# Storing the last tile of a fused attention and feed-forward kernel by column halves

## The chip, the core and the metric

The kernel runs on one core of a Trainium2 chip. A core has a matrix engine (PE, TensorE) with its own queue for weight loads (PEld), a vector engine (DVE), a scalar engine (ACT), GpSimd (POOL) and a queue engine (SP, SyncE). PE writes its results to PSUM, in banks of 128 partitions by 512 float32. DVE and ACT read PSUM and write SBUF. DMA transfers move data between SBUF and HBM; here they are issued from SP's queue and, a few of them, from ACT's queue, and they run on the core's 16 DMA engines. The metric is the device time of one execution in microseconds (us), the median of several runs.

## The reference

A small attention (8 batches, 8 heads, 576 tokens, 64 channels) over 32 learned slots per head is followed by a feed-forward layer with an ELU:

```python
def _attn_ref(q, k, v, phi):
    a = softmax(phi, axis=2)                      # over the 576 tokens
    k_m = np.einsum('bhsm,bhsd->bhmd', a, k)      # 32 slots per head
    v_m = np.einsum('bhsm,bhsd->bhmd', a, v)
    attn = softmax(q @ k_m.T / 8, axis=-1)
    return attn @ v_m

def _moe_ref(x, w_in, w_out):                     # x: 4608 x 512
    h = x @ w_in                                  # 512 -> 2048
    g = np.where(h > 0.0, h, np.exp(np.minimum(h, 0.0)) - 1.0)
    return g @ w_out                              # 2048 -> 512
```

## The kernel before, in words

The tokens of a batch are worked on in two halves of 288. `hidden` makes 128 of the 2048 feed-forward channels for one half (a PSUM tile `psh` of 128 x 288), ACT and DVE apply the ELU, and `project` multiplies the result by 128 rows of `w_out` and adds it up over the 16 groups of channels (j = 0 to 15) in PSUM banks `pso`. Every product is made of three passes over high and low parts of the operands (`PASSES`), to keep float32 precision; `by_channels` issues the three matmuls of one group.

A half has 288 tokens, that is two tiles of 128 (NT = 2) and 32 left over (REST). `project` takes the two tiles. The 32 left-over tokens are gathered: two batches, two halves each, make 4 x 32 = 128 rows, one full tile `rest` for each pair of batches (p = 0 to 3). When a pair is through, eight units (i = 0 to 7) run, each for two groups of channels: `rest_high` (ACT) and `rest_low` (DVE) split the values into high and low parts `gp`, and `rest_project` (PE) issues six matmuls of 128 x 512 into one bank, `pso00`. `rest_store` then copies the bank to an SBUF tile `orest` on ACT and stores it to `out`. Its 128 rows lie in `out` as four blocks of 32 rows (batch b, half h), each block contiguous, the blocks 288 rows apart. The stores of p = 0, 1 and 2 stand in the middle of the program, that of p = 3 is the last thing that the kernel does.

The order is written by hand: the list `FIRST` for the first part and a table of places (`at(place, step, ...)`, sorted by place) for the rest; each engine runs its instructions in that order. For the last pair, the eight units stand at it + 0.612 to it + 0.682, the copies of the last two ordinary tiles (`collect`) at it + 0.7, their store at it + 0.8 and `rest_store` at it + 0.81.

Two other lines matter for the reading. `store` (L950) writes two ordinary tiles with one transfer of 128 partitions (512 KB). `spread_max` (L282) sends eight rows of 128 B to a DRAM tile `nmd`; its destination is written as four rows of two pieces (`d.rearrange("a r x -> r a x")`, that is 4 x 2 x 32 elements).

Of the kernel before, what the change touches and what calls it, by code (L numbers as in the profile page):

```python
# [12 lines left out]
ALU = mybir.AluOpType  # L13
# [3 lines left out]
P = 128  # L17
B, H, S, D, M = 8, 8, 576, 64, 32
DM, DFF = 512, 2048
HALF = S // 2  # L20
NT = HALF // P
REST = HALF - NT * P
# [9 lines left out]
NJ = DFF // P  # L32
# [142 lines left out]
def fused_kernel(ctx: ExitStack, tc: tile.TileContext, phiT, phi, kv0, kvt, kv, kvb, q0, q1, w_in, w_out, out):  # L175
# [8 lines left out]
    nc = tc.nc  # L184
# [13 lines left out]
    wout = {}  # L198
    def t2k(shape, name):
        return work.tile(shape, F32, name=name, tag="t2k", bufs=7)  # L200
# [47 lines left out]
    def bank(shape, where):  # L248

        pool, name = {  # L250
            "b": (ps_b, "psb"), "h": (ps_h, "psh"),
            "w": (ps_o, "pso00"), "x": (ps_o, "pso01"),
            "y": (ps_o, "pso10"), "z": (ps_o, "pso11"),
        }[where]
        return pool.tile(shape, F32, name=name)
# [578 lines left out]
    gs = {}  # L834
# [75 lines left out]
    acc = {}  # L910
    osbs = {}

    def by_channels(ps, gp, j, first, last):
        for n, (x, y) in enumerate(PASSES):
            nc.tensor.matmul(  # L915
                ps,
                gp[:, y],
                wout[j][:, x, :],
                start=(first and n == 0),
                stop=(last and n == 2),  # L920
            )

    def project(it):
        b, hf, j = order[it]
        _, first, last = ends[it]
        if first:
            acc[b, hf] = [ps_o.tile([P, DM], F32, name=f"pso{hf}{t}") for t in range(NT)]
        gp = gps.pop(it)
        for t in range(NT):
            by_channels(acc[b, hf][t], gp[:, :, t * P : (t + 1) * P], j, first, last)  # L930
# [31 lines left out]
    def rest_low(p, i):  # L962
# [2 lines left out]
            gp[:, LO], gf.rearrange("p j n -> p (j n)"), gp[:, HI], ALU.subtract  # L965
        )

    def rest_project(p, i):
        if i == 0:
            acc["rest", p] = ps_o.tile([P, DM], F32, name="pso00")  # L970
        gp = gs.pop(("rest", p, i))[1]
        for n in range(2):
            j = 2 * i + n
            by_channels(acc["rest", p], gp[:, :, n * P : (n + 1) * P], j, j == 0, j == NJ - 1)

    def rest_store(p):
        t = t2k([P, DM], "orest")
        nc.scalar.copy(t, acc.pop(("rest", p)))

        eng = (nc.sync, nc.scalar) if p == B // 2 - 1 else (nc.sync, nc.sync)  # L980
        for n in range(4):
            eng[n % 2].dma_start(
                out[2 * p + n // 2, n % 2, NT * P :], t[n * REST : (n + 1) * REST, :]
            )

    tiny = work.tile([P, 1], F32, name="tiny", bufs=1)
    work.tile([P, 24], F32, name="pad_tiny", bufs=1)
# [22 lines left out]
    def warm_up(n):  # L1010
# [8 lines left out]
        for f in (  # L1019
# [4 lines left out]
            softmax_divide, back, turn_back, probs_high, probs_low, vw, vw_high, vw_low, hidden,  # L1024
            elu_exp, elu_max, elu_rest, rest_copy, elu_high, elu_low, project, collect, store, rest_high, rest_low,
            rest_project, rest_store,
        )
    }
    words = {"K": (0,), "V": (1,), "KV": (0, 1)}
    first = []  # L1030
# [9 lines left out]
    def at(place, f, *a):  # L1040
        if (f, a) not in done:
            plan.append((place, len(plan), f, a))
# [84 lines left out]
    for it, (b, hf, j) in enumerate(order):  # L1127
        o = it - 1.35 if it in behind else it - 1.7
        if b > NB:
            o -= 0.96 * (it % 2)  # L1130
        at(o, hidden, it)
        at(o + 0.01, elu_exp, it)
        at(o + 0.02, elu_max, it)
        if b < NB:
            at(it - 1.67, rest_copy, it)
        elif b > NB and b % 2 == 0 and order[max(it - 2, 0)][0] != b:
            at(32 * b - 0.34 + 0.005 * (it - 32 * b), elu_rest, it)
        else:
            at(o + 0.03, elu_rest, it)
        late = 0.695 if it and b != order[it - 1][0] and b % 2 == 0 and b > NB else 0  # L1140
        at(it - 1 + late, elu_high, it)
        at(it - 0.99 + late, elu_low, it)
        at(it + 0.6, project, it)
        if ends[it][2]:
            for t in range(NT):
                at(it + 0.7, collect, it, t)
            if j == NJ - 1:
                at(it + 0.8, store, b, hf)
                if b % 2 and hf:
                    for i in range(NJ // 2):  # L1150
                        at(it + 0.61 + 0.01 * i, rest_high, b // 2, i)
                        at(it + 0.611 + 0.01 * i, rest_low, b // 2, i)
                        at(it + 0.612 + 0.01 * i, rest_project, b // 2, i)
                    at(it + 0.81, rest_store, b // 2)

    plan.sort(key=lambda x: x[:2])
# [50 lines left out]
```

## Time and profile before

| | us |
|---|---|
| median of 3 runs (701.78 to 702.86) | 702.29 |
| the profiled execution | 702.28 |
| its span, from the first to the last instruction | 700.3 |
| PE busy in it | 690.1 |
| DVE, ACT, POOL busy | 460.1, 445.5, 66.2 |

The profiled execution's time is 1.98 us longer than its span. The profile lists the instructions by engine and source line, the waits between them, the chain of work that ended last, and the packets of the DMA engines: a packet is one contiguous piece that one engine moves, or the 4-byte write with which an engine reports that its part of a transfer is done. The share of the DMA engines is an average over all 16.

### The profile page before, as it was taken

Reading aid. Unit: us, or ns where it says so; the run is one execution under the profiler, and the core shown is the slowest. Engines: PE = TensorE matmul, PEld = TensorE weight load, DVE = VectorE, ACT = ScalarE, POOL = GpSimd, SP = SyncE. Lnnn points to the kernel's source line nnn. Section 1 sums busy time; section 2 is a strip of 40 time slices with the busy share of each in tenths; the row PEclk is TensorE's granted clock in tenths of the full one; section 3 lists DMA queues with packets and bytes.
Section 4 is the critical chain, followed back from the end, with each engine's and each line's share of the span. In section 5 each row is a group of like instructions: output and inputs, shape, how many; then the busy total and the mean of one; then the engine's idle time right before and its main releaser. Section 6 shows DMA issues by size and latency. Waiting matters only on the chain.

```text
span 700.3 us, 14400 instructions
## 1 busy us (share of the span) xinstructions
PE 690.1 (99%) x5496; PEld 579.7 (83%) x5496; DVE 460.1 (66%) x1264; ACT 445.5 (64%) x1106; POOL 66.2 (9%) x111
## 2 busy tenths in 40 slices
PE   8999999999999999999999999999999999999997
PEld 7778887888868888888887887888888888878886
DVE  4989887977696558576664666766674655766442
ACT  3879988877457576656655566655664555666552
POOL 0332352123001010001000010000100000000000
PEclk9999999999999999999999999999999999999999
DMA  9992014341404451123202232030501200000001
GB/s 337 407 364 91 1 42 143 101 146 42 137 31 134 168 181 47 49 85 120 85 1 60 90 112 92 31 103 3 174 29 46 69 1 31 1 31 1 30 1 46
DMA packets 24220, 64.14 MB, mean 92 GB/s; under 512 B 3288, under 2 KB 4824, under 8 KB 24152
## 3 DMA queue, kind: packets, MB, share of 16 engines
q1 hardware_dynamic: 23480, 63.06, 25.8%
q8 instruction: 44, 0.72, 0.4%
q10 hardware_dynamic: 672, 0.16, 0.1%
q14 instruction: 24, 0.20, 0.1%
HBM read 53.77 MB, written 9.44 MB: 90 GB/s over the span
## 4 chain that ended last, share of the span: by engine, by line
PE 94%; DMA 4%; DVE 0%; issue 0%; ACT 0%; SPq 0%
PE pso L915 57%; PE psh L854 29%; PE psb L578 3%; PE psb L505 2%; DMA raw<-w_out 2%; PE pso L578 2%; DMA raw<-w_in 1%; PE psh L578 1%; DMA qh<-q 1%; DMA touch<-kv 0%; PE psb L591 0%; PE pso L591 0%; PE psb L547 0%; PE psh L734 0%; SPq L321 0%
## 5 line engine op out<-in xcount | busy, mean ns | idle before, releaser
L915 PE MATMUL pso<-wout,gp 128*128 128x512 f32 x1728 | 426.8, 393 | 0.0
L915 PEld LDWEIGHTS pso<-wout,gp 128*128 128x128 f32 x1728 | 314.2, 188 | 66.5 <-issue 4.0
L854 PEld LDWEIGHTS psh<-A,vw 128*128 128x128 f32 x1536 | 218.4, 188 | 19.4 <-DVE gp L907 2.5
L854 PE MATMUL psh<-A,vw 128*128 128x288 f32 x1536 | 230.4, 295 | 0.7 <-ACT A L777 0.4
L869 ACT ACTIVATE gf<-psh 128x288 f32<-128x288 f32 x256 | 104.6, 409 | 120.8 <-PE psh L854 118.0
L881 DVE SCALAR_TENSOR_TENSOR gf<-gf,psh 128x256 f32<-128x256 f32 x192 | 80.3, 418 | 115.9 <-ACT gf L870 115.8
L907 DVE TENSOR_TENSOR gp<-gf,gp 128x256 fp32r<-128x256 f32 x256 | 113.2, 445 | 29.0 <-ACT gp L901 27.0
L901 ACT CAST gp<-gf 128x256 fp32r<-128x256 f32 x256 | 101.5, 401 | 34.1 <-DVE gf L881 17.3
L870 ACT ACTIVATE gf<-gf 128x288 f32<-128x288 f32 x256 | 113.9, 445 | 8.1
L293 POOL TENSOR_TENSOR e<-e,nmb 128x512 f32<-128x512 f32 (+1 forms) x18 | 19.1, 1081 | 291.9 <-DMA e<-phi 97.6
L878 DVE SCALAR_TENSOR_TENSOR gf<-gf,psh 128x288 f32<-128x288 f32 x64 | 28.5, 450 | 17.1 <-ACT gf L870 15.4
L889 DVE SCALAR_TENSOR_TENSOR rest<-gf,psh 128x32 f32<-128x32 f32 x192 | 34.6, 180 | 0.0
L816 DVE TENSOR_TENSOR vw<-psb,vw 128x512 fp32r<-128x512 f32 (+2 forms) x40 | 20.9, 561 | 14.3 <-ACT vw L810 14.3
L959 ACT CAST gp<-rest 128x256 fp32r<-128x256 f32 x32 | 13.0, 406 | 25.1 <-PE pso L915 25.1
L964 DVE TENSOR_TENSOR gp<-rest,gp 128x256 fp32r<-128x256 f32 x32 | 13.3, 421 | 18.8 <-ACT gp L959 18.5
L897 POOL COPY rest<-gf 128x32 f32<-128x32 f32 x64 | 18.7, 319 | 71.2 <-DVE gf L878 71.2
L810 ACT CAST vw<-psb 128x512 fp32r<-128x512 f32 (+2 forms) x40 | 17.5, 488 | 11.8 <-PE psb L578 11.6
L395 ACT ACTIVATE mag<-raw 128x512 uint32<-128x512 uint32 x30 | 20.0, 669 | 2.7 <-DVE win L417 1.4
L391 ACT ACTIVATE mag<-raw 128x512 f32<-128x512 f32 x30 | 19.7, 667 | 1.3 <-DMA raw<-w_in 1.0
L578 PE MATMUL psb<-win,kvm 64*32 64x512 f32 (+2 forms) x320 | 17.9, 505 | 0.0
L816 DVE TENSOR_TENSOR vw<-pso,vw 128x512 fp32r<-128x512 f32 (+1 forms) x18 | 10.1, 597 | 9.9 <-ACT vw L810 9.8
L505 PEld LDWEIGHTS psb<-kvt,e 64*32 64x32 f32 x864 | 12.6, 105 | 3.3 <-issue 3.3
(144 smaller groups left out, 474.1 us busy)
## 6 DMA issues: line engine op xcount, KB each, us to landing
kvt<-kvb SPq DMA_DIRECT2D x24, 512.0 KB, 4.8
raw<-w_in SPq DMA_DIRECT2D x15, 512.0 KB, 8.0
raw<-w_out SPq DMA_DIRECT2D x15, 512.0 KB, 10.0
out<-osb SPq DMA_DIRECT2D x14, 512.0 KB, 2.8
qt<-q SPq DMA_DIRECT2D x18, 384.0 KB, 4.3
kvt<-kv SPq DMA_DIRECT2D x8, 512.0 KB, 8.9
ph<-phiT SPq DMA_DIRECT2D x7, 576.0 KB, 5.6
e<-phi SPq DMA_DIRECT2D x12, 256.0 KB, 3.4
```

The lines of the kernel that those rows point to most:

```text
L505: nc.tensor.matmul(ps[a][32 * j : 32 * j + 32], e[r, 32 * j : 32 * j + 32], t[r, k % 2, :, j], start=(k == 0), stop=(k == NBL - 1), tile_p ...
L578: nc.tensor.matmul(outs[a][32 * j : 32 * j + 32, :], lhs[r, 32 * j : 32 * j + 32], rhs[r, j], start=True, stop=True, tile_position=(64 * a ...
L816: nc.vector.tensor_tensor(t[:, LO, a, n0:n1], s["ps"]["vw", c, n0][a], t[:, HI, a, n0:n1], ALU.subtract)
L854: nc.tensor.matmul(ps, t[:, x, g, c0 : c0 + P], s["A"][hf][:, y, g, :], start=(n == 0), stop=(n == 5),)
L869: nc.scalar.activation(gf, ps, AF.Relu, scale=-1.0)
L870: nc.scalar.activation(gf, gf, AF.Exp, scale=-1.0)
L878: nc.vector.scalar_tensor_tensor(gf, gf, -1.0, ps, ALU.add, ALU.max)
L881: nc.vector.scalar_tensor_tensor(gf[:, :n], gf[:, :n], -1.0, ps[:, :n], ALU.add, ALU.max)
L889: nc.vector.scalar_tensor_tensor(rest_of(b, j)[:, o : o + REST], gf[:, n:], -1.0, ps[:, n:], ALU.add, ALU.max)
L901: nc.scalar.copy(gp[:, HI], gs[it][:, : NT * P])
L907: eng.tensor_tensor(gp[:, LO], gf[:, : NT * P], gp[:, HI], ALU.subtract)
L915: nc.tensor.matmul(ps, gp[:, y], wout[j][:, x, :], start=(first and n == 0), stop=(last and n == 2),)
```

## The change

The stores of p = 0, 1 and 2 become one transfer of 128 rows instead of four of 32. Its destination is a view of `out` with three dimensions, 4 x 32 x 512.

For the last pair, units 0 to 6 add up in `pso00` as before. The last unit (i = 7, groups 14 and 15) is moved behind the copies and the store of the ordinary tiles. ACT copies the sums of groups 0 to 13 from `pso00` to `orest`. PE then makes the last two groups by column halves, columns 256 to 511 first, each half with six matmuls of 128 x 256 into a bank `psh` of its own, and DVE adds each half to the copied sums. The first half leaves by one transfer on SP's queue (destination 4 x 32 x 256); the second leaves by two transfers of 64 rows (destination 2 x 32 x 256), one on SP's and one on ACT's queue.

```diff
--- before.py
+++ after.py
@@ -910,12 +910,12 @@
     acc = {}
     osbs = {}
 
-    def by_channels(ps, gp, j, first, last):
+    def by_channels(ps, gp, j, first, last, n0=0, n1=DM):
         for n, (x, y) in enumerate(PASSES):
             nc.tensor.matmul(
                 ps,
                 gp[:, y],
-                wout[j][:, x, :],
+                wout[j][:, x, n0:n1],
                 start=(first and n == 0),
                 stop=(last and n == 2),
             )
@@ -965,23 +965,43 @@
             gp[:, LO], gf.rearrange("p j n -> p (j n)"), gp[:, HI], ALU.subtract
         )
 
+    HALF_DM = DM // 2
+
     def rest_project(p, i):
         if i == 0:
             acc["rest", p] = ps_o.tile([P, DM], F32, name="pso00")
-        gp = gs.pop(("rest", p, i))[1]
-        for n in range(2):
-            j = 2 * i + n
-            by_channels(acc["rest", p], gp[:, :, n * P : (n + 1) * P], j, j == 0, j == NJ - 1)
+        gp = gs["rest", p, i][1]
+        ps = acc["rest", p]
+        of = [(2 * i + n, gp[:, :, n * P : (n + 1) * P]) for n in range(2)]
+        if p < B // 2 - 1 or i < NJ // 2 - 1:
+            last = NJ - 1 if p < B // 2 - 1 else NJ - 3
+            for j, g in of:
+                by_channels(ps, g, j, j == 0, j == last)
+            return
+
+        t = t2k([P, DM], "orest")
+        nc.scalar.copy(t, ps)
+        for n in (1, 0):
+            half = bank([P, HALF_DM], "h")
+            cols = slice(n * HALF_DM, (n + 1) * HALF_DM)
+            for j, g in of:
+                by_channels(half, g, j, j == 2 * i, j == NJ - 1, cols.start, cols.stop)
+            nc.vector.tensor_tensor(t[:, cols], half, t[:, cols], ALU.add)
+            if n:
+                nc.sync.dma_start(rest_rows(p)[:, :, cols], t[:, cols])
+            else:
+                rows = slice(0, P // 2), slice(P // 2, P)
+                for eng, r, h in ((nc.sync, rows[0], slice(0, 2)), (nc.scalar, rows[1], slice(2, 4))):
+                    eng.dma_start(rest_rows(p)[h, :, cols], t[r, cols])
+
+    def rest_rows(p):
+        return out[2 * p : 2 * p + 2, :, NT * P :].rearrange("b h r n -> (b h) r n")
 
     def rest_store(p):
-        t = t2k([P, DM], "orest")
-        nc.scalar.copy(t, acc.pop(("rest", p)))
-
-        eng = (nc.sync, nc.scalar) if p == B // 2 - 1 else (nc.sync, nc.sync)
-        for n in range(4):
-            eng[n % 2].dma_start(
-                out[2 * p + n // 2, n % 2, NT * P :], t[n * REST : (n + 1) * REST, :]
-            )
+        if p < B // 2 - 1:
+            t = t2k([P, DM], "orest")
+            nc.scalar.copy(t, acc["rest", p])
+            nc.sync.dma_start(rest_rows(p), t)
 
     tiny = work.tile([P, 1], F32, name="tiny", bufs=1)
     work.tile([P, 24], F32, name="pad_tiny", bufs=1)
@@ -1150,7 +1170,8 @@
                     for i in range(NJ // 2):
                         at(it + 0.61 + 0.01 * i, rest_high, b // 2, i)
                         at(it + 0.611 + 0.01 * i, rest_low, b // 2, i)
-                        at(it + 0.612 + 0.01 * i, rest_project, b // 2, i)
+                        last = 0.2 if b + 1 == B and i == NJ // 2 - 1 else 0
+                        at(it + 0.612 + 0.01 * i + last, rest_project, b // 2, i)
                     at(it + 0.81, rest_store, b // 2)
 
     plan.sort(key=lambda x: x[:2])
```

The end of PE's program, from the last matmuls of unit 6 on (`wout_2083` and `wout_2164` are the weights of groups 14 and 15), before:

```order
L915 MATMUL pso_8463<-wout_1649,gp 128x512 x3
L915 MATMUL pso_8463<-wout_1793,gp 128x512 x3
L915 MATMUL pso_8463<-wout_1894,gp 128x512 x3
L915 MATMUL pso_8463<-wout_2114,gp 128x512 x3
L915 MATMUL pso_8463<-wout_2083,gp 128x512 x3
L915 MATMUL pso_8463<-wout_2164,gp 128x512 x3
```

and now:

```order
L915 MATMUL pso_8454<-wout_1894,gp 128x512 x3
L915 MATMUL pso_8454<-wout_2114,gp 128x512 x3
L915 MATMUL psh<-wout_2083,gp 128x256 x3
L915 MATMUL psh<-wout_2164,gp 128x256 x3
L915 MATMUL psh<-wout_2083,gp 128x256 x3
L915 MATMUL psh<-wout_2164,gp 128x256 x3
```

Six matmuls of 128 x 512 have become twelve of 128 x 256, in two banks; nothing ahead of them on PE has moved.

The end of SP's queue, from the last batch's loads and small transfers on (L282 is the transfer to `nmd`; the last size is that of the destination as the instruction carries it), before:

```order
L282 DMA nmd<-nmb 4x2x32
L285 DMA nmb<-nmd 64x128 x2
L271 DMA e<-phi 128x512 x2
L271 DMA e<-phi 128x128
L950 DMA out<-osb 128x2x512
L306 DMA kvt<-kvb 128x1024 x4
L306 DMA kvt<-kvb 128x512
L950 DMA out<-osb 128x2x512
L982 DMA out<-orest 32x512 x4
L338 DMA qt<-q 128x768 x3
L950 DMA out<-osb 128x2x512 x4
L982 DMA out<-orest 32x512 x2
```

and now, from the store of p = 2 on:

```order
L1004 DMA out<-orest 4x32x512
L338 DMA qt<-q 128x768 x3
L950 DMA out<-osb 128x2x512 x4
L991 DMA out<-orest 4x32x256
L995 DMA out<-orest 2x32x256
```

The four transfers of a middle store have become one, and the two last ones of SP have other shapes; ACT's queue, which had two transfers of 32 x 512 at its end, now has one of 2 x 32 x 256.

## Rows read from the trace of the kernel before

**Rows 1.** The page: span, PE's busy time and the chain's shares by engine

```profile
span 700.3 us, 14400 instructions
...
PE 690.1 (99%) x5496; PEld 579.7 (83%) x5496; DVE 460.1 (66%) x1264; ACT 445.5 (64%) x1106; POOL 66.2 (9%) x111
...
PE 94%; DMA 4%; DVE 0%; issue 0%; ACT 0%; SPq 0%
```

**Rows 2.** The chain that ended last, 665 to 701: start us, us, what

```profile
678.17 1.56 PE psh L854 x12
679.73 16.52 PE pso L915 x72
696.24 0.02 issue
696.27 0.58 ACT orest L978
```

**Rows 3.** Timeline, 680 to 701: start us, us, engine line op tiles

```profile
692.12 0.41 ACT L959 CAST gp<-rest 128x256 fp32r<-128x256 f32 x1 [0.98 <-PE pso L915]
692.44 0.58 ACT L945 COPY osb<-pso 128x512 f32<-128x512 f32 x1
692.56 0.43 DVE L964 TENSOR_TENSOR gp<-rest,gp 128x256 fp32r<-128x256 f32 x1 [0.97 <-ACT gp L959]
692.90 0.68 DVE L947 COPY osb<-pso 128x512 f32<-128x512 f32 x1
...
696.27 0.58 ACT L978 COPY orest<-pso 128x512 f32<-128x512 f32 x1 [3.25 <-PE pso L915]
696.88 0.80 SPq L982 DMA_DIRECT2D out<-orest  x2
696.88 0.85 ACTq L982 DMA_DIRECT2D out<-orest  x2
```

**Rows 4.** DMA view, 697.5 to 699: engines' share in 40 slices, packets, queues

```profile
DMA  0000096885924499929972389896976995022000
...
DMA packets 192, 0.26 MB, mean 175 GB/s; under 512 B 64, under 2 KB 64, under 8 KB 192
...
q10 hardware_dynamic: 96, 0.13, 40.0%
q1 hardware_dynamic: 96, 0.13, 31.4%
```

**Rows 5.** DMA view, 163 to 164.8, with one transfer alone

```profile
DMA  0000000000000000000000000000000100000000
...
DMA packets 12, 0.00 MB, mean 1 GB/s; under 512 B 12, under 2 KB 12, under 8 KB 12
...
nmd<-nmb SPq DMA_DIRECT2D x1, 1.0 KB
```

**Rows 6.** DMA view, 536.5 to 539, with one store of two ordinary tiles

```profile
DMA packets 272, 0.52 MB, mean 210 GB/s; under 512 B 16, under 2 KB 16, under 8 KB 272
...
q1 hardware_dynamic: 272, 0.52, 55.8%
```

**Rows 7.** DMA view, 374 to 378, with the four stores of p = 1

```profile
DMA packets 192, 0.26 MB, mean 66 GB/s; under 512 B 64, under 2 KB 64, under 8 KB 192
...
out<-orest SPq DMA_DIRECT2D x4, 64.0 KB, 1.7
```

**Rows 8.** Issues of the small transfer on SP: all six, and one in the timeline

```profile
L282 SPq DMA_DIRECT2D nmd<-nmb x6: 572/582/671, 163.1 to 486.5; - x6
...
163.11 0.67 SPq L282 DMA_DIRECT2D nmd<-nmb  x1
```

**Rows 9.** DMA view, 164.8 to 167, with transfers of 512 B rows

```profile
DMA packets 104, 0.04 MB, mean 20 GB/s; under 512 B 19, under 2 KB 104, under 8 KB 104
...
q1 hardware_dynamic: 104, 0.04, 6.9%
```

**Rows 10.** Groups on DVE, 640 to 700: count, busy us, mean ns

```profile
L881 DVE SCALAR_TENSOR_TENSOR gf<-gf,psh 128x256 f32<-128x256 f32 x20 | 8.4, 422 | 21.8 <-ACT gf L870 21.8
```

**Rows 11.** Waits, 200 to 700, those that a DMA ended: us, times, longest

```profile
POOL e L293 <- DMA e<-phi: 97.6, 2, 73.7
```

**Rows 12.** Timeline, 209 to 250: the first middle store, the load behind it, its reader

```profile
209.80 1.99 SPq L982 DMA_DIRECT2D out<-orest  x4
...
211.83 0.43 SPq L265 DMA_DIRECT2D ph<-phiT  x1
...
218.86 1.35 DVE L449 TENSOR_REDUCE nm<-ph 128x2 f32<-128x1152 f32 x1
```

## The prediction, made before the changed kernel ran

> **What bounds the kernel now.** I read the page first. PE is busy for 690.1 of 700.3 us and the chain that ended last is 94% PE [rows 1], so for most of the span only PE counts. The change leaves PE's order alone up to its last six matmuls; what it can move is the tail. The chain in order of time shows that tail: a run of `pso` matmuls to 696.24, and ACT's copy of the bank to 696.85 [rows 2]. The timeline goes on: SP and ACT each issue two transfers from 696.88 on, the last issue ending at 697.73 [rows 3]. The DMA view shows packets from 697.69 (slice 6 of 40, each 0.0375 us) to 698.89 (slice 37) [rows 4]. So the first packet comes 0.81 us after the first issue begins, and from the last packet to the end of the span (completion, the final waits) it is 700.3 - 698.89 = 1.41 us. All that lies between the last matmul and the end is 4.06 us. The reader should ask of the change which of these pieces it shortens, and whether it lengthens the packet phase, which is now 1.20 us.
>
> **How many engines a transfer uses** is the question behind it. An engine reports its part of a transfer by one 4-byte packet, so the small packets count the engines. A store of two ordinary tiles has 256 rows of 2 KB and 272 packets, 16 of them small: 16 engines [rows 6]. The four middle stores of 32 rows have 128 rows and 64 small packets: again 16 each [rows 7]. But the transfer to `nmd`, eight rows of 128 B into a destination written as 4 x 2 x 32, leaves 12 packets in all: eight rows and only four reports [rows 5]. It runs on four engines, although eight rows would have allowed eight. What it has that the others lack is a leading destination dimension of 4. The new transfers have just that form: 4 x 32 x 512 for the middle stores, 4 x 32 x 256 for the first half, and 2 x 32 x 256 for the two last ones. Read from that row, they run on four, four, and two engines. The Trainium skill states such a rule (DMA: Bandwidth & Descriptors, section Why a DMA increments its semaphore by 16 and not by 1): the count is the largest number up to 16 that divides the slowest dimension of both sides, and the engines taken are the lowest-numbered. The 12 packets agree with its first part; which engines are taken no row shows. By both parts together the sum is the one below.
>
> **The change part by part**, in the clock of the profiled execution (702.28 us, 1.98 outside its span; it is the median of the runs within 0.01).
>
> PE: 16.52 us for 72 matmuls is 0.229 each [rows 2], so groups 0 to 13 end at 696.24 - 6 x 0.229 = 694.87. A matmul of 256 columns is not in the trace. From below it is half of 0.229, 0.115; the nearest row is 12 of 288 columns in 1.56 us, 0.130 each [rows 2]; from above it is 0.229, if the repeated weight loads set the pace. I take 0.115, which the 288-column row scales to. The first half ends at 695.56, the second at 696.25, where PE ended before: the split costs PE nothing (at 0.130 it is +0.18, at 0.229 +1.38).
>
> ACT copies the bank at 694.90 for 0.58 [rows 3], to 695.48, hidden under the first half's matmuls by 0.08 us. The casts and copies ahead of it on ACT and DVE end at about 693.6 [rows 3], so they block nothing.
>
> DVE adds: 128 x 256 from PSUM and SBUF, as L881, 0.42 [rows 10]; bounds 0.42 and the 0.68 of the 512-column copy [rows 3]. The first half is ready at 695.56 + 0.03 + 0.42 = 696.01, the second at 696.70.
>
> Issues: with four engines the trace has one case, 0.58 us of SP (0.67 the first time) [rows 8], and its first packet shows at 164.39 (slice 32, 0.045 us each), 1.28 us after the issue began at 163.11 [rows 5, 8]. From below it is the 0.81 us of the old stores. I take 1.28, the row of the same form. The first half's issue at 696.03 gives packets from 697.31; SP is free again at 696.61, before the second half is ready, and both queues issue at 696.73, with packets possible from 698.01.
>
> Packets: a row is now 1 KB, which the trace lacks. A 2 KB row costs 55.8% x 2.5 us x 16 / 272 = 82 ns of one engine [rows 6]; in the window with 512 B rows a packet costs 6.9% x 2.2 us x 16 / 104 = 23 ns [rows 9]. On the line between them 1 KB is 23 + 59/3 = 43 ns; bounds 23 and 82. I take 43. Load per engine: the first half puts 128 / 4 = 32 rows on each of four engines, each last transfer 64 / 2 = 32 rows on each of two. If all three begin at the same engine, two engines carry 96 rows, 96 x 43 ns = 4.13 us, without a gap, since 32 rows (1.38 us) last until 698.69, past 698.01. They end at 697.31 + 4.13 = 701.44. That is 2.55 us later than the last packet before (698.89). The 1.41 us behind it stay. Sum: 702.28 + 2.55 = 704.83.
>
> What the change gains is real but off this path: 0.16 us of the copy against the add, 0.4 us of a second issue. The first half's earlier start only lets the two loaded engines begin sooner.
>
> Middle stores: three times SP issues once instead of four times, 1.99 us the first time [rows 12], against 0.58; and four engines carry 32 rows of 2 KB each, 32 x 82 ns = 2.6 us. Behind the first stands a load issued at 211.83, whose reader starts at 218.86 [rows 12]. After 200 us no wait of PE, ACT or DVE ends with a DMA; only POOL's do, and POOL is busy for 9% of the span [rows 11, 1]. I take zero. If that cover were gone, each store could cost its 2.6 us less the 1.4 that SP saves, 1.2, three times 3.6 us; below zero there is nothing to win, as nothing waits for these transfers.
>
> **The rivals.**
>
> *All engines after all* (not slower). If the compiled transfer is cut by its rows and not by its leading dimension, 16 engines share 256 rows of 1 KB. The second half is issued at 696.73, its packets start 0.81 later at 697.54 and need 8 x 43 ns = 0.34, to about 697.95 with the reports; the end moves by 697.95 - 698.89 = -0.94: 701.3. It decides wherever the three transfers use 16 engines. For it: every large transfer of the trace does [rows 6, 7]. Against it: the one transfer with a leading 4 doesn't [rows 5].
>
> *Other engines for the queues.* Few engines per transfer, but ACT's two are not SP's. Then the fullest engines carry 64 rows, 2.75 us from 697.31, to 700.06: +1.17, 703.45. No row of before excludes it; the old last stores, two on each queue, filled all 16 engines together (71% of them over 1.5 us [rows 4]) and say nothing on this. I keep same engines as likelier: it needs no memory of what went before.
>
> *A row costs as much as a 2 KB row.* 96 x 82 ns = 7.87 us, to 705.18: +6.29, 708.6. For it: the packets of the last stores cost 89 ns on the mean, small ones included [rows 4], so something besides bytes may count. Against it: the 512 B rows at 23 ns.
>
> The Trainium skill also has a rule on halves (same page, section Rules for kernel authors): two transfers of disjoint partition halves share the same 16 engines, so only the issue time is saved. It speaks against the last split; by it alone the time would be that of the first rival, since the issue saved is counted there. The trace agrees as far as it goes: the old last stores' packets from both queues share the engines at the same time [rows 4].
>
> **How the numbers follow.** Forecast, few and shared engines at 43 ns or near it: 0.70, 704.8, its own range 704.0 to 706.2 (first packet at 0.81 us instead of 1.28 takes 0.5 off; PE at 0.229 adds 0.7; 50 ns for a row adds 0.7). All engines: 0.10, 701.3. Other engines: 0.10, 703.4. Rows at up to 82 ns: 0.10, up to 708.6. A range from 703.2 to 707.4 leaves out the first rival and about half of the last, some 17%. A measurement of this kernel can't tell less than 0.2%, 1.4 us, from no change. So slower by more than that (over 703.7) has the forecast and the last rival, 0.80, and a bit of the other-engines case, 0.02; faster (below 700.9) has only what is left of the first rival if its end comes earlier still, 0.02; the same 0.16.
>
> **What would show it.** In the DMA view of the tail: 256 rows and 4 + 2 + 2 = 8 small packets, 264 in all (304 by the first rival), a share of the 16 engines of 0.25 at first and then of 0.13 or so for several us, and a last packet near 701.4. PE should still end near 696.25, ACT's copy should lie before the first add, and DVE's adds take 0.42 each. In the middle, each store should leave 132 packets with no new wait on PE. I am wrong if the small packets of the tail number 48, if the last two transfers end soon after 698, or if PE ends much after 696.4.

## The result and the profile after

The changed kernel takes 706.18 us (median of 6, 706.04 to 707.26) against 701.80 for the kernel before in the same runs: ratio 1.0063, 95% interval 1.0051 to 1.0076, slower. The profiled execution took 706.16 us, 3.88 more than that of before.

The page, to be held against [rows 1]:

```profile
span 704.0 us, 14404 instructions
...
PE 690.2 (98%) x5502; PEld 580.4 (82%) x5502; DVE 460.9 (65%) x1266; ACT 445.3 (63%) x1106; POOL 66.0 (9%) x111
...
PE 93%; DMA 4%; DVE 1%; issue 0%; ACT 0%; SPq 0%
```

PE is busy as long as before; the span is 3.7 us longer. The chain that ended last, in order of time (start us, us, what), to be held against [rows 2]:

```profile
679.69 15.12 PE pso L915 x66
694.81 1.45 PE psh L915 x12
696.26 0.02 issue
696.28 0.42 DVE orest L989
```

PE ends at 696.26, before at 696.24: twelve half-wide matmuls take 1.45 us, 0.121 each, and the whole loss lies behind them. The timeline of the tail (start us, us, engine line op tiles), to be held against [rows 3]:

```profile
694.85 0.59 ACT L983 COPY orest<-pso 128x512 f32<-128x512 f32 x1 [1.87 <-PE pso L915]
695.63 0.42 DVE L989 TENSOR_TENSOR orest<-psh,orest 128x256 f32<-128x256 f32 x1 [2.09 <-PE psh L915]
696.09 0.59 SPq L991 DMA_DIRECT2D out<-orest  x1
696.28 0.42 DVE L989 TENSOR_TENSOR orest<-psh,orest 128x256 f32<-128x256 f32 x1 [0.22 <-PE psh L915]
696.77 0.53 SPq L995 DMA_DIRECT2D out<-orest  x1
696.78 1.36 ACTq L995 DMA_DIRECT2D out<-orest  x1
```

The copy lies under the matmuls, the last data are ready at 696.70, and the last issues begin at 696.77, earlier than the last ones of before. What follows is in the DMA view from 697 to 703 (share of the 16 engines in 40 slices of 0.15 us, packets, queues), to be held against [rows 4]:

```profile
DMA  0022212222222211200111011101111111110000
...
DMA packets 264, 0.26 MB, mean 44 GB/s; under 512 B 8, under 2 KB 264, under 8 KB 264
...
q1 hardware_dynamic: 198, 0.20, 12.1%
q10 hardware_dynamic: 66, 0.07, 3.1%
```

q1 is SP's queue, q10 ACT's. SP's 198 packets are 128 + 64 rows and 6 reports, ACT's 66 are 64 rows and 2: four engines for the first transfer and two for each of the others. The same stretch by half microseconds (window, its length, busy us of PE, PEld, DVE, ACT, POOL, PE's clock, DMA share, GB/s):

```profile
697.00:697.50 0.50, 0.00 (x0) 0.00 (x0) 0.00 (x0) 0.00 (x0) 0.00 (x0) 1.00 0.11 18
697.50:698.00 0.50, 0.00 (x0) 0.00 (x0) 0.00 (x0) 0.00 (x0) 0.00 (x0) 1.00 0.22 43
698.00:698.50 0.50, 0.00 (x0) 0.00 (x0) 0.00 (x0) 0.00 (x0) 0.00 (x0) 1.00 0.27 86
...
699.50:700.00 0.50, 0.00 (x0) 0.00 (x0) 0.00 (x0) 0.00 (x0) 0.00 (x0) 0.50 0.08 29
...
701.50:702.00 0.50, 0.00 (x0) 0.00 (x0) 0.00 (x0) 0.00 (x0) 0.00 (x0) 0.50 0.13 47
```

The share is about 4/16 at first and then 2/16 to the end. (A packet's whole time is counted in the stretch in which it starts, so single slices can show more or less than that.) Rows move from 697.3 to about 702.6, 5.3 us instead of 1.2.

### The profile page after: what moved, and what is told of

It reads as the page before. It is cut to its first block, busy times and chain, and to the rows that moved or that the text cites. A ratio compares the mean times of both kernels' runs of the same rounds, so it can differ in the third digit from the quotient of the medians.

```text
span 704.0 us, 14404 instructions
## 1 busy us (share of the span) xinstructions
PE 690.2 (98%) x5502; PEld 580.4 (82%) x5502; DVE 460.9 (65%) x1266; ACT 445.3 (63%) x1106; POOL 66.0 (9%) x111
## 4 chain that ended last, share of the span: by engine, by line
PE 93%; DMA 4%; DVE 1%; issue 0%; ACT 0%; SPq 0%
PE pso L915 56%; PE psh L854 29%; PE psb L578 3%; PE psb L505 2%; DMA raw<-w_out 2%; PE pso L578 2%; DMA raw<-w_in 1%; PE psh L578 1%; DMA qh<-q 1%; DMA touch<-kv 0%; PE psb L591 0%; PE pso L591 0%; PE psb L547 0%; PE psh L915 0%; PE psh L734 0%
```

## The experiments

PE's end differs by about a microsecond between the profiled executions (695.60 to 696.72), so besides the ratio each profile gives the tail: its span less PE's end (the row "issue" of its chain). Before it is 700.3 - 696.24 = 4.06 us, after 704.0 - 696.26 = 7.74.

| kernel | us | before beside it | ratio, 95% interval | tail, us |
|---|---|---|---|---|
| e1 blocks of 32 rows | 702.15 | 702.34 | 0.9997 (0.9988 to 1.0007) | 3.87 |
| e2 middle stores only | 702.33 | 702.34 | 1.0003 (0.9993 to 1.0012) | 4.1 |
| e3 last store in one | 705.62 | 702.34 | 1.0051 (1.0034 to 1.0067) | 7.7 |
| e4 last half on four | 704.32 | 702.34 | 1.0030 (1.0019 to 1.0040) | 5.7 |
| e5 all on SP | 705.62 | 702.23 | 1.0045 (1.0030 to 1.0061) | 7.8 |
| e6 rows interleaved | 701.97 | 702.23 | 0.9997 (0.9989 to 1.0006) | 3.8 |
| e7 interleaved, whole | 702.02 | 702.23 | 0.9999 (0.9990 to 1.0007) | 4.4 |
| e8 two units by halves | 701.90 | 702.14 | 0.9999 (0.9990 to 1.0008) | 3.5 |

**e1, blocks of 32 rows.** The changed kernel with other transfers, nothing else:

```diff
-            if n:
-                nc.sync.dma_start(rest_rows(p)[:, :, cols], t[:, cols])
-            else: ...
+            for m in range(4):
+                eng = (nc.sync, nc.scalar)[m // 2]
+                eng.dma_start(out[2 * p + m // 2, m % 2, NT * P :, cols],
+                              t[m * REST : (m + 1) * REST, cols])
```

> The changed kernel, but the two halves of the last tile leave by transfers of one block of 32 rows each (destination 32 x 256), for each half two on SP and two on ACT. Rows are still 1 KB and the halves still come one after the other. Theory (few engines): with 32 rows leading, each transfer runs on 16 engines; 8 x 16 = 128 small packets in the tail; the four issues of 0.4 us on each queue end near 697.7 as before, the last packet comes near 698.7, so about 701.8 (701.3 to 702.3). Rival 1 (rows of 1 KB or the halving itself are the cost): still over 704. Rival 2 (the middle stores cost it): unchanged at 706.2, since they stay as in the changed kernel.

Measured: 702.15, as the kernel before. The issues and the DMA view from 696 to 699 (slices of 0.075 us):

```profile
695.65 1.75 SPq L992 DMA_DIRECT2D out<-orest  x4
695.66 1.80 ACTq L992 DMA_DIRECT2D out<-orest  x4
```
```profile
DMA  0000002598620587730488640377840000000000
...
DMA packets 384, 0.26 MB, mean 88 GB/s; under 512 B 128, under 2 KB 384, under 8 KB 384
```

There are 128 small packets for eight transfers, 16 each, and shares up to 0.9; the last packet is at 698.3. Rows are still 1 KB, the halves and the middle stores are those of the changed kernel, and the loss is gone. Rivals 1 and 2 fall.

**e2, the middle stores alone.** The kernel before with

```diff
+        if p < B // 2 - 1:
+            nc.sync.dma_start(out[2 * p : 2 * p + 2, :, NT * P :].rearrange("b h r n -> (b h) r n"), t)
+            return
...
```

> The kernel before with only the three middle stores as one transfer of 4 x 32 x 512 each. Theory (few engines, but only the tail counts): as before, 701.8, within 0.5, although each store leaves 132 packets and takes over 2.5 us. Rival (middle stores cost through the loads behind them): 1 to 4 us more, with waits of PE, ACT or DVE on a DMA after 200 us.

Measured: 702.33, no difference within an interval of -0.5 to +0.8 us. That the stores did become long shows in the DMA view from 538.6 to 544.6 (slices of 0.15 us), around the store of p = 2:

```profile
DMA  0000000012630090010122212222222222211000
...
DMA packets 132, 0.26 MB, mean 44 GB/s; under 512 B 4, under 2 KB 4, under 8 KB 132
```

Four small packets, so four engines, and rows from about 539.8 to 544.3. The only wait after 200 us that a DMA ended is again POOL's:

```profile
POOL e L293 <- DMA e<-phi: 181.8, 3, 84.4
```

It is longer than in [rows 11], and still costs nothing that the times show. The middle stores do not matter.

**e3, the last store in one transfer.** The kernel before with `out[...]` of four blocks as one 4 x 32 x 512 on SP, in place of the four transfers of 32 x 512.

> The kernel before, but its last store is one transfer of 4 x 32 x 512 on SP: rows of 2 KB, no halves, nothing on ACT. Theory (few engines): 132 packets in the tail, four engines with 32 rows each at 84 to 107 ns, so 2.7 to 3.4 us from about 698.1, the last packet at 700.8 to 701.5 instead of 698.89, 703.7 to 704.4 us. Rival 1 (1 KB rows or the halving are the cost): 701.4 to 701.8, since one issue replaces two.

Measured: 705.62, slower as expected, but by more. The DMA view from 697 to 703 (slices of 0.15 us):

```profile
DMA  0000126300900101222122222222222110000000
...
DMA packets 132, 0.26 MB, mean 44 GB/s; under 512 B 4, under 2 KB 4, under 8 KB 132
```

Four small packets: four engines, with 2 KB rows, no halves and nothing on ACT. Rows move from 697.6 to 702.1, 4.5 us for 32 rows an engine, where 2.7 to 3.4 were expected. Two stretches of it (columns as in the windows above) show why:

```profile
697.70:699.30 1.60, 0.00 (x0) 0.00 (x0) 0.00 (x0) 0.00 (x0) 0.00 (x0) 0.52 0.25 23
...
700.00:702.00 2.00, 0.00 (x0) 0.00 (x0) 0.00 (x0) 0.00 (x0) 0.00 (x0) 0.50 0.23 91
```

In both the share is that of four busy engines (4/16), but in the first 1.6 us they move 23 GB/s, later 91. So the zeros in the view are not idle engines: single rows take very long there. The digits from the first packet on (126300900) are those of the middle store in e2, so this slow start comes with the transfer and not with the end of the program. Of the 3.3 us by which the rows last longer than the 1.2 us of before, the count of engines with the 2.7 us expected makes 1.5; the slow start makes the other 1.8.

**e4, the last half on four engines.** The changed kernel with one transfer of 4 x 32 x 256 on SP for each half:

```diff
-            if n: ...
-            else: ...
+            nc.sync.dma_start(rest_rows(p)[:, :, cols], t[:, cols])
```

> The changed kernel, but the second half leaves by one transfer of 4 x 32 x 256 on SP instead of two of 2 x 32 x 256 on SP and ACT. Theory (few engines, the same for every transfer): four engines carry 64 rows each instead of two with 96, at the 55 ns that a row took in the changed kernel (697.30 to 702.56 for 96) 3.5 us, at 43 ns 2.8: the last packet at 700.1 to 700.8, 1.8 to 2.5 us earlier, 703.7 to 704.4. Rival 2 (ACT's long issue of 1.36 us and its late packets are the cost): the SP part ended at 701.15 in the changed kernel, so 704.8 or more.

Measured: 704.32, the tail 2.0 us shorter than the changed kernel's. The DMA view from 697 to 703:

```profile
DMA  0000132122222312232323222200000000000000
...
DMA packets 264, 0.26 MB, mean 44 GB/s; under 512 B 8, under 2 KB 264, under 8 KB 264
```

The rows take from 697.6 to 700.9, 3.3 us for 64 an engine, 52 ns each. The time goes with the rows on the fullest engine: 64 instead of 96.

**e5, all on SP.** `(nc.scalar, rows[1], ...)` becomes `(nc.sync, rows[1], ...)`.

> The changed kernel, but both last transfers of 2 x 32 x 256 are issued on SP, none on ACT. Theory (few engines, the same for both queues): two engines still carry 96 rows, so 706.2, within 0.5; the share of the 16 engines stays at 0.13 to the end. Rival 2 (ACT's issue of 1.36 us and its late packets cost the time): the last packet a microsecond or more earlier, 704.0 to 705.2.

Measured: 705.62, 0.6 below what was expected and so just outside the 0.5 allowed; the interval overlaps that of the changed kernel, and the tail is 7.8 us. The DMA view from 697 to 703:

```profile
DMA  0013212222222212101111011011111111110000
```

Again 2/16 to the end at 702.7. So ACT's long issue (1.36 us) cost nothing that can be seen, and moving ACT's transfer behind SP's made nothing longer, as is to be expected if it ran on the two engines of SP's anyway. The last section shows that it did.

**e6, rows interleaved.** The gathered rows in the order 4 r + block, so that a store's destination has 32 or 16 leading:

```diff
-        return rests[p, i][:, j % 8, :]
+        x = rests[p, i][:, j % 8, :].rearrange("p (r k) -> p k r", k=4)
+        return x[:, b % 2 * 2 + hf, :]
...
-        return out[2 * p : 2 * p + 2, :, NT * P :].rearrange("b h r n -> (b h) r n")
+        return out[2 * p : 2 * p + 2, :, NT * P :].rearrange("b h r n -> r (b h) n")
```

> The changed kernel with the rows of the gathered tile in another order: row = 4 r + block instead of 32 block + r, so that the destinations of its stores have 32 (or 16) leading instead of 4 (or 2). Halves, banks, queues and the count of transfers are those of the changed kernel. Theory (few engines): every store on 16 engines, 48 small packets in the tail; the second half's issue at 696.77, packets from 697.6 for 0.4 to 0.7 us, last packet at 698.0 to 698.3, 0.6 to 0.9 us before that of the kernel before: 700.9 to 701.3. Rival 1 (halving or 1 KB rows cost): over 704. Strided writes of the gathered rows may cost DVE and POOL some time, without moving PE.

Measured: 701.97, the same as before; the tail is 0.26 us shorter, not 0.6 to 0.9. Issues, and the DMA view from 696 to 699:

```profile
695.62 0.58 SPq L992 DMA_DIRECT2D out<-orest  x1
...
696.30 0.57 SPq L996 DMA_DIRECT2D out<-orest  x1
696.32 0.65 ACTq L996 DMA_DIRECT2D out<-orest  x1
```
```profile
DMA  0000000000039899630035669595200000000000
...
DMA packets 304, 0.26 MB, mean 87 GB/s; under 512 B 48, under 2 KB 304, under 8 KB 304
```

48 small packets, 16 engines for each transfer, so the theory holds for the engines. But the second burst begins in slice 21, at 697.5, 1.2 us after its issues began; I had reckoned with about 0.8. The expectation fails there.

**e7, interleaved without halves.** The kernel before with e6's rows and one transfer of 64 rows on each queue.

> The kernel before with the rows in the order of e6 and no halves: the last tile leaves by one transfer of 64 rows of 2 KB on each queue (destination 16 x 4 x 512), the middle stores by one each. Theory: 16 engines each, one issue per queue instead of two saves 0.4 us, the last packet near 698.4 to 698.5: 701.3 to 701.5. If this equals e6, the column halves gain nothing; if e6 is 0.2 to 0.4 us faster, that is what they bring once the engines are right.

Measured: 702.02, the same as before and not the 701.3 to 701.5 expected, the tail 0.3 us longer. Issues, and the DMA view from 697 to 700:

```profile
697.35 0.59 SPq L986 DMA_DIRECT2D out<-orest  x1
697.35 0.65 ACTq L986 DMA_DIRECT2D out<-orest  x1
```
```profile
DMA  0000000000000000000005579499987765300000
...
DMA packets 160, 0.26 MB, mean 87 GB/s; under 512 B 32, under 2 KB 32, under 8 KB 160
```

One issue a queue less saved nothing: the first rows come at 698.6, 1.2 us after the issue. On 16 engines the same 256 KB in rows of 2 KB last 1.1 us (698.6 to 699.7), in e3 on four engines 4.5, so most of e3's slow start goes with the few engines too. Against e7, the halves bring 0.6 us of tail in the profile once the engines are right; against the kernel before, 0.26. The times (702.02 and 701.97 in e6) show neither.

**e8, two units by halves.** e1 with units 6 and 7 by halves, so that the first half's four issues are over when the second half is ready:

```diff
+        if end and i == NJ // 2 - 2:
+            return
+        of = [(2 * u + n, gs["rest", p, u][1][:, :, n * P : (n + 1) * P])
+              for u in ((i - 1, i) if end and i == NJ // 2 - 1 else (i,)) for n in range(2)]
...
-            last = NJ - 1 if p < B // 2 - 1 else NJ - 3
+            last = NJ - 5 if end else NJ - 1
```

> The kernel of e1 (blocks of 32 rows, two per queue and half) with the last two units by column halves instead of the last one, so that the first half is ready 1.45 us before PE ends and its four issues no longer stand in front of the second half's. Theory (engines right, then only the issues and the latency behind them count): from PE's end, add at 0.45, two issues per queue from 0.48, the second's packets from about 1.8, last packet at 2.1 instead of 2.5 in e1 and 2.7 in the kernel before; from there 1.4 to the end: a tail of 3.5 us against 3.9 and 4.0, so 0.5 us faster than before, about 0.07%. Rival (the tail is held by something else, as the engines' own pace or a wait of the end): 3.9 as in e1.

Measured: the tail is 3.5 us, as expected, by this chain and a span of 699.1:

```profile
692.71 2.89 PE psh L915 x24
695.60 0.02 issue
695.62 0.42 DVE orest L995
```

It is the shortest tail of all. In the times it is 701.90 against 702.14, ratio 0.9999 (0.9990 to 1.0008): a gain of 0.5 us cannot be told from none here. No version was shown to beat the kernel before.

## Why the prediction was right, and which term was too small

The direction, the mechanism and the range held: 704.8 was forecast, range 703.2 to 707.4, and 706.18 measured. It lies at the upper end of the forecast's own range (704.0 to 706.2), which allowed for 50 ns a row and not for the 55 found, so part of the closeness is luck. By the steps:

- PE's end: 696.25 forecast, 696.26 in the profile. The half-wide matmul takes 0.121 us, between the 0.115 taken and the 0.130 of the nearest row.
- Copy and adds: 694.90 and 0.42 forecast, 694.85 and 0.42 measured; the copy is hidden.
- Issue and first packet: 0.58 and 1.28 forecast from the transfer to `nmd` [rows 5, 8]; 0.59 on SP, first rows at 697.3 where 697.31 was forecast. ACT's issue took 1.36, which was not foreseen and, by e5, cost nothing.
- Engines: four, two and two, as read from the 12 packets of one transfer [rows 5]. The rule of the Trainium skill (DMA: Bandwidth & Descriptors, section Why a DMA increments its semaphore by 16 and not by 1) gives the same counts, and e6, whose destinations lead with 32 and 16, shows its other side: 48 small packets, 16 engines. Its other part, that the engines taken are the lowest-numbered, would put both queues on the same ones; that they share them is shown in the last section, which numbers they have no view tells.
- The mis-sized term is the packet phase: "96 x 43 ns = 4.13 us, without a gap". It lasted from 697.3 to 702.6, 5.3 us, 55 ns a row. The 43 was right for steady rows: at 47 GB/s on two engines 1 KB takes 43.6 ns, in the window from 701.5. What was left out are stretches of slow rows, two above all:

```profile
697.30:698.00 0.70, 0.00 (x0) 0.00 (x0) 0.00 (x0) 0.00 (x0) 0.00 (x0) 1.00 0.23 42
...
699.00:701.10 2.10, 0.00 (x0) 0.00 (x0) 0.00 (x0) 0.00 (x0) 0.00 (x0) 0.50 0.13 35
```

Four engines move 42 GB/s in the first, where they move 86 from 698 on, and two move 35 in the second instead of 47, while the share stays that of busy engines. Against those rates the first stretch loses about 0.4 us and the second about 0.5, most of the 1.2 us by which 5.3 lies over 4.13. The engines are busy without a gap, as forecast; it is the time of a row that was too small. The profiled time (706.16) lies 1.33 above the sum (704.83): these 1.2, and mainly time outside the span, 2.16 us instead of 1.98.

- The end behind the last packet: 1.41 forecast, 704.0 - 702.6 = 1.4 measured.
- Middle stores: zero, within the interval of e2. The store shown there runs on four engines as forecast, but for about 4.5 us instead of 2.6, and nothing waits for it.
- "What the change gains is real but off this path": shown in part, by one profile each and not by the times. With the engines right, the halves shorten the tail by 0.2 (e1) and 0.26 us (e6), less than the 0.9 of the first rival, since in e1 four issues stand in each queue and in e6 the latency of 1.2 us stays.

The rivals: all engines after all, refuted by the eight small packets; other engines for the queues, refuted by the hand-over in the last section; a row of 1 KB as dear as one of 2 KB, refuted by the 43.6 ns of the steady rows. The rule of the Trainium skill about two disjoint halves (same page, section Rules for kernel authors) speaks of halves that use all 16 engines, which these did not; here the issue time saved was worth nothing, since the issues were not the bound.

What stays open is why rows on few engines are slow in stretches, mostly at the start. It is seen in the changed kernel, in e3 (1.6 us at 23 GB/s), in the middle stores of e2 and, weaker, in e4; no run varied it alone.

## What to carry to other kernels

Before merging stores of several blocks into one transfer, look at the leading dimension of both sides, and count the small packets of such a transfer in the trace: 128 or 64 rows behind a leading 4 or 2 ran on four or two engines, and at the end of a program that time is all exposed. Interleaving the rows so that a multiple of 16 leads, or plain transfers of 32 rows, gives the engines back. Then reckon the tail as add, issue, latency to the first row, rows, and completion; with all engines the rows (0.7 us for the last ones in e6, 1.2 in the kernel before) take less than the 1.4 us behind the last packet, and splitting the data brought at most 0.5 us of tail here (e8), too little to be seen in the times.

## What the runs showed that was not expected

The latency from an issue to its first row does not go with the count of engines. It is 1.2 us in e3 and e4 (four engines) and just as much in e6 and e7 (16 engines), all of whose destinations are cut otherwise than their source (128 rows against 4 x 32 or 32 x 4), and their issues take 0.57 to 0.65 us. It is 0.8 for the stores of 32 x 512, alike on both sides [rows 3, 4], with issues of about 0.4. The number of rows does not go with it: the store of two ordinary tiles in the kernel before, 256 rows cut alike on both sides, is issued in 0.37 us, and its first packets show in slice 21 of the DMA view from 693 to 696, at 694.5, about 0.85 us after the issue began:

```profile
693.65 0.37 SPq L950 DMA_DIRECT2D out<-osb  x1
```
```profile
DMA  0000000000000000000059998999999989999961
```

The form of the transfer goes with it in all runs; that it is the cause was not tried by itself.

ACT's rows did not take turns with SP's; they waited for them, on the same two engines. 188 of the 192 rows of SP's queue started before 701.1. These are the queues in the stretch from 701.1 to 703 of the changed kernel:

```profile
q10 hardware_dynamic: 66, 0.07, 9.7%
q1 hardware_dynamic: 6, 0.00, 0.7%
```

The 66 packets of ACT's queue are all that it has in the tail, although its issue had ended at 698.14. The hand-over is in the DMA view from 701.14 to 701.24 (slices of 2.5 ns):

```profile
DMA  2009900000000000000099000000000000000920
...
DMA packets 7, 0.01 MB, mean 51 GB/s; under 512 B 2, under 2 KB 7, under 8 KB 7
...
q10 hardware_dynamic: 3, 0.00, 8.6%
q1 hardware_dynamic: 4, 0.00, 6.9%
```

The two 2s are the reports of SP's two engines. About 10 ns behind the first one a row of ACT's starts, the first of all; while SP's other engine makes its last two rows, ACT's come one at a time, 42 ns apart. Engines of its own would not have had to wait for SP's reports.
